# Sparse attention and a gated feed-forward layer on one core: attention products by 64 rows of one head, with dense keys and values

## The chip, the cores and the metric

The kernel runs on one NeuronCore of a Trainium2 chip. The core has five engines with a queue of instructions each: PE (TensorE, the matrix products; its weight loads are shown apart as PEld), DVE (VectorE), ACT (ScalarE), POOL (GpSimd) and SP (SyncE, which here only starts DMAs). PE writes into PSUM, which has 8 banks of 2 KB in each of 128 partitions. The metric is the device time of one execution in microseconds (us). Each number below is from three executions or from one profiled execution.

## What is computed

Eight batches, eight heads, 576 tokens, 64 numbers per head. In heads 0 to 3 a query sees the 32 tokens up to itself ("local"), in heads 4 to 7 the tokens whose position has the same remainder by 32 ("strided"). The result, 4608 tokens of 512 numbers, goes through a layer with 2048 hidden units:

```python
scores = scale * np.matmul(q, k.transpose(0, 1, 3, 2))
mask_local = (rel >= 0) & (rel < stride)                       # stride = 32
mask_strided = (rel >= 0) & (pos[None, :] % stride == pos[:, None] % stride)
scores = np.where(masks, scores, -1e9); attn = softmax(scores)
x = np.matmul(attn, v)                     # back to tokens x 512
h = x @ w_in
out = (h * (1 / (1 + np.exp(-h)))) @ w_out
```

## The kernel before

**Attention.** Two heads of one kind go together. A batch has six groups: three local (12 tiles of 32 queries, of both heads) and three strided (8, 8 and 6 tiles of 54 queries: three remainders of 18 tokens). A group has these steps, with the letters used below: S, the scores (L357, PE); M, mask, maximum and sign (L373, DVE), with the exponentials (L380, ACT; in the first two batches U on POOL, L389, and E on ACT, L393); R, sums and reciprocals (L398 to L400, DVE), and N, the scaling of a strided group (L404, DVE); T, transposes of 128x128 (L410, PE), and P, their copy to SBUF (L414, ACT); O, the products with the values (L422 local, L430 strided, PE). A local group goes on with Q, the division (L440, DVE), X, three transposes back (L460, PE), and B, a copy into `xb` (L465, ACT); of a strided group B sorts straight out of PSUM into `xb` (L453, ACT).

Both heads lie on the 128 partitions, and the keys and the values of a tile are spread out as a block diagonal with zeros: `kbd` is 128 x (2 x 64), and one product of 128 rows gives the scores of both heads. The zeros are written once at the start (L193 to L198 on DVE and POOL, L201 on ACT), and only then may keys and values be loaded between them, by two DMAs each (L315, L321). The output of a local product lies on 32 of PE's columns, that of a strided one on 64, so four or two of them, with different columns, can be under way at once. In float32 a product leaves two records in the trace (two weight loads and two matmuls), a transpose one.

**Feed-forward.** Nine blocks of 512 tokens, each of 16 chunks of 128 hidden units. A chunk is 12 matmuls of `hidden` (L492), tanh and gate (L502, L506), a split into a high and a low part (L514, L518), and 12 matmuls of `output` (L538), which come one chunk later. Every number is split into two float32r parts, and three products of them are summed. The input `x` of a block is split the same way (L480, L484) into one tile for each half, with a single place: the split of the next block stands after the last `hidden` of a block.

**Order.** PE's order is the program's. The first part (attention of batches 0 and 1, block 0, and the splitting of the weights, which arrive as 8-byte floats in 32 pieces of 512 KB) is put in order by a planner (`Steps.arrange`), which gives each step a cost per engine and a due time, and counts PSUM places ("rings"). From block 1 on the order is written out: after six of a block's 16 chunks `between` does T of group c+1, X of group c-1, S of group c+2, O of group c, R of group c+2. All of these and `hidden` take their PSUM banks in turn from a pool of four (`ps`); the other four (`po`) hold the sums of `output`. The groups of a batch run in the order local, local, local, strided, strided, strided.

Of the kernel before, what the change touches and what calls it, by code (L numbers as in the profile page):

```python
# [28 lines left out]
P = 128  # L29
# [11 lines left out]

KW = 64
# [4 lines left out]
VBUFS = 2  # L47

# [3 lines left out]


# [27 lines left out]


# [3 lines left out]
SIGNAL = 0.2  # L86

# [9 lines left out]
class Steps:  # L97
# [27 lines left out]
    def ready(self, step):  # L125
# [6 lines left out]
        for ring in step.takes:  # L132
            if len(self.taken[ring]) >= self.rings[ring]:
                for other in self.taken[ring][-self.rings[ring]].ends[ring]:
# [3 lines left out]
        return at  # L138

    def arrange(self):  # L140
        free = collections.defaultdict(float, SP=1.3, DVE=6.0, ACT=7.6, POOL=6.8)
        left, order = list(self.all), []
        while left:
# [9 lines left out]
            step.start, step.end, step.cost = at, at + cost, cost  # L153
            free[step.engine] = step.end
# [8 lines left out]
def sparse_attention_ffn(ctx: ExitStack, tc: tile.TileContext, kqt, vt, w_in, w_out, out):  # L163
# [12 lines left out]
        (1, 0, 12): "stage0", (1, 0, 14): "stage1", (1, 1, 12): "stage2", (1, 1, 14): "stage3",  # L176
        (1, 0, 9): "vbd2", (1, 1, 9): "zeros", (1, 0, 7): "kbd2",
# [8 lines left out]
    const.tile([P, 64], F32, name="pad1")  # L186
    zeros = const.tile([P, VT * D], F32, name="zeros")
# [11 lines left out]
    for vbd in vbds[1:]:  # L199
        for h in range(2):  # L200
            nc.scalar.copy(out=vbd[:, h], in_=zeros)  # L201
    vbds = [vbd.rearrange("p h (t d) -> p h t d", d=D) for vbd in vbds]
# [26 lines left out]
    make_identity(nc, ident)  # L229
# [5 lines left out]
    const.tile([P, 96], F32, name="pad3")  # L235
# [5 lines left out]
    def weight(layer, half, fc):  # L241
# [4 lines left out]
        if key not in places:  # L246
            places[key] = const.tile([P, n, DM], F32R, name=lent.get(key, "w%d%d_%d" % key))
# [64 lines left out]
    def load_qk(b, gi):  # L312
        n = max(GROUPS[gi].nq, GROUPS[gi].nk)
        for h in range(2):
# [3 lines left out]
    def load_v(b, gi):  # L318
        n = GROUPS[gi].count
        for h in range(2):  # L320
            load(out=vbds[gi % (VBUFS if b else VBUFS + 1)][h::2, h, :n], in_=vt[b, gi, h::2, :n])  # L321

# [7 lines left out]
    class Attention:  # L330


        def __init__(self, b, gi):
            self.b, self.gi, self.g = b, gi, GROUPS[gi]
            g = self.g
            self.kbd = kbds[gi % (KBUFS if b else KBUFS + 1)]
            self.vbd = vbds[gi % (VBUFS if b else VBUFS + 1)]
# [6 lines left out]
            self.quick = NG * b + gi < 2 * NG + 2  # L344
# [6 lines left out]

        def scores(self):
            g, kbd = self.g, self.kbd
            self.pss = self.bank("pss")
            s_ps = self.pss.rearrange("p (c h k) -> p c h k", h=2, k=KW)
# [143 lines left out]
    def tanh(ph, cols=slice(0, T), th=None):  # L499
        if th is None:  # L500
            th = ffn.tile([P, T], F32, name="th", bufs=1)
# [346 lines left out]
```

## Time and profile before

| | us |
|---|---|
| median of three executions (lowest, highest) | 936.03 (935.22, 936.04) |
| the profiled execution, its own time | 937.39 |
| its span from first to last instruction | 935.6 |
| PE busy | 916.1 (98%) |
| DVE busy | 431.8 (46%) |
| ACT busy | 322.6 (34%) |
| POOL busy | 19.0 (2%) |
| the chain of work that ended last: on PE | 91% |
| mean clock granted to PE, of full speed | 0.992 |

The profile is of one execution, and its own time lies 1.4 us above the median. A duration of one matmul (390 ns) is longer than the distance to the next one (227 ns), since matmuls overlap; so a stretch of PE's work is measured from its first start to the next stretch's first start. [...]

### The profile page before, as it was taken

What the parts mean: (1) busy time and instruction counts of PE and PEld (TensorE: products, weight loads), DVE (VectorE), ACT (ScalarE), POOL (GpSimd) and SP (SyncE); (2) the same over time, 40 slices, a digit from 0 to 9 for tenths busy, and PEclk for the clock granted to TensorE, in tenths of its full rate; (3) what the DMA queues carried; (4) which work ended last, traced back from release to release, by engine and by line L of the source; (5) the groups of instructions that cost most, each with busy time, mean ns of one, the idle gap of its engine ahead of it and who ended that gap; (6) DMA issues with size and microseconds to landing.
All of it is one profiled execution on the core that took longest, in us unless ns stands there. A gap on an engine that the chain in (4) does not pass through costs nothing.

```text
span 935.6 us, 15127 instructions
## 1 busy us (share of the span) xinstructions
PE 916.1 (98%) x5896; PEld 747.7 (80%) x5896; DVE 431.8 (46%) x1379; ACT 322.6 (34%) x915; POOL 19.0 (2%) x39
## 2 busy tenths in 40 slices
PE   6899999999999999999999999999999999999997
PEld 4687878888888888888888888888888888888886
DVE  7898754533544444433444344434343343343332
ACT  4877633323423233223432252233332131112112
POOL 4001000000000000000000000000000000000000
PEclk9799999999999999999999999999999999999999
DMA  7875522101301112102211121011210010001001
GB/s 237 287 254 182 179 77 82 57 29 45 109 27 39 56 37 94 45 29 72 82 48 38 36 91 55 30 58 44 82 38 9 1 46 1 1 0 46 1 1 45
DMA packets 36486, 62.85 MB, mean 67 GB/s; under 512 B 4160, under 2 KB 23616, under 8 KB 36416
## 3 DMA queue, kind: packets, MB, share of 16 engines
q1 hardware_dynamic: 36416, 61.90, 20.5%
q8 instruction: 46, 0.75, 0.3%
q14 instruction: 24, 0.20, 0.1%
HBM read 52.45 MB, written 9.44 MB: 66 GB/s over the span
## 4 chain that ended last, share of the span: by engine, by line
PE 91%; DVE 3%; DMA 3%; ACT 2%; issue 0%; SPq 0%; ACTq 0%
PE ps L492 41%; PE po L538 39%; PE ps L357 4%; PE ps L430 2%; PE ps L422 2%; DMA kbd<-kqt 2%; PE ps L410 2%; DVE xlo L484 1%; DMA stage<-w_in 1%; PE ps L460 1%; DVE glo L518 1%; ACT th L502 0%; ACT xhi L480 0%; DVE ghi L514 0%; ACT stage L256 0%
## 5 line engine op out<-in xcount | busy, mean ns | idle before, releaser
L492 PE MATMUL ps<-xhi,w 128*128 128x512 f32 x1152 | 387.6, 396 | 1.8 <-ACT pt L414 1.8
L506 DVE SCALAR_TENSOR_TENSOR th<-th,ps 128x512 f32<-128x512 f32 (+1 forms) x147 | 99.4, 676 | 350.1 <-ACT th L502 349.2
L492 PEld LDWEIGHTS ps<-xhi,w 128*128 128x128 f32 x1152 | 217.2, 189 | 51.8 <-issue 3.2
L502 ACT ACTIVATE th<-ps 128x512 f32<-128x512 f32 (+1 forms) x147 | 86.5, 589 | 459.6 <-PE ps L492 457.9
L492 PE MATMUL ps<-xlo,w 128*128 128x512 f32 x576 | 226.3, 393 | 0.3
L538 PE MATMUL po<-w,ghi 128*128 128x512 f32 x576 | 183.5, 390 | 0.4 <-DVE ghi L514 0.4
L492 PEld LDWEIGHTS ps<-xlo,w 128*128 128x128 f32 x576 | 108.7, 189 | 24.8 <-DVE xlo L484 3.4
L538 PEld LDWEIGHTS po<-w,ghi 128*128 128x128 f32 x576 | 108.0, 188 | 23.1 <-DVE ghi L514 0.6
L518 DVE TENSOR_TENSOR glo<-th,ghi 128x512 fp32r<-128x512 f32 (+1 forms) x147 | 100.1, 681 | 11.1 <-ACT ghi L514 0.4
L538 PE MATMUL po<-w,glo 128*128 128x512 f32 x252 | 98.2, 390 | 0.5 <-DVE glo L518 0.5
L538 PE MATMUL po<-stage,ghi 128*128 128x512 f32 x288 | 88.7, 389 | 0.0
L380 ACT ACTIVATE sm<-sm,sums 128x64 f32<-128x64 f32 x228 | 76.8, 341 | 17.3 <-DVE sums L373 17.3
L514 DVE CAST ghi<-th 128x512 fp32r<-128x512 f32 (+1 forms) x138 | 58.1, 421 | 11.3 <-PE po L538 0.5
L538 PEld LDWEIGHTS po<-stage,ghi 128*128 128x128 f32 x288 | 54.1, 188 | 11.4
L538 PE MATMUL po<-stage,glo 128*128 128x512 f32 x144 | 56.1, 390 | 0.0
L538 PEld LDWEIGHTS po<-w,glo 128*128 128x128 f32 x252 | 47.3, 188 | 10.8 <-DVE glo L518 0.9
L357 PE MATMUL ps<-kbd 128*32 128x128 f32 (+1 forms) x928 | 47.8, 292 | 8.0 <-POOL ident masks.py:197 5.1
L357 PEld LDWEIGHTS ps<-kbd 128*32 128x32 f32 (+1 forms) x928 | 35.0, 125 | 17.8 <-issue 11.1
L414 ACT COPY pt<-ps 128x384 f32<-128x384 f32 (+1 forms) x42 | 21.6, 513 | 79.4 <-PE ps L410 79.4
L380 ACT ACTIVATION_READ_ACCUMULATOR sm<-sm,sums 128x1 f32 x228 | 42.9, 188 | 0.0
L373 DVE CUSTOM_DVE_ANT_0 sm<-ps,mask_strided 128x64 f32<-128x64 f32 x176 | 27.3, 220 | 33.3 <-PE ps L357 33.3
L538 PE MATMUL po<-vbd,ghi 128*128 128x512 f32 x108 | 42.1, 390 | 0.0
(81 smaller groups left out, 769.7 us busy)
## 6 DMA issues: line engine op xcount, KB each, us to landing
vbd<-vt SPq DMA_DIRECT2D x48, 192.0 KB, 3.3
out<-osb SPq DMA_DIRECT2D x36, 256.0 KB, 2.1
stage<-w_in SPq DMA_DIRECT2D x16, 512.0 KB, 4.4
stage<-w_out SPq DMA_DIRECT2D x16, 512.0 KB, 4.8
kbd<-kqt SPq DMA_DIRECT2D x32, 221.0 KB, 3.3
kbd<-kqt SPq DMA_DIRECT2D x32, 208.0 KB, 3.0
vbd<-vt SPq DMA_DIRECT2D x32, 128.0 KB, 2.7
kbd<-kqt SPq DMA_DIRECT2D x16, 224.0 KB, 3.2
```

The costliest lines, as they stand in the source:

```text
L357: nc.tensor.matmul(s_ps[rows, c], kbd[:, 1, g.q0[t] : g.q0[t] + g.rows], kbd[:, 0:3:2, g.k0[t] : g.k0[t] + KW], start=True, stop=True,)
L373: nc.vector.tensor_tensor_reduce(out=s_sb[:, c, h], in0=s_ps[:, c, h], in1=masks[g.local, g.starts[c]][:, :KW], scale=-SCALE, scalar=BIG, ...
L380: nc.scalar.activation(out=s_sb[:, c, h], in_=s_sb[:, c, h], func=AF.Exp, bias=nmax[:, c, h : h + 1], scale=-1.0, accum_out=rsum[:, c, h : ...
L410: nc.tensor.transpose(self.psp[:, at], self.sm[:, at], ident)
L414: nc.scalar.copy(out=self.pt[:, : self.cols], in_=self.psp[:, : self.cols])
L422: nc.tensor.matmul(o_ps[rows, c], pt[:, c * P + rows.start : c * P + rows.stop], vbd[:, :, t], start=True, stop=True,)
L492: nc.tensor.matmul(ph, weight(0, wi, fc)[:, cc * P : (cc + 1) * P], x[xi][:, cc], start=(cc, n) == (0, 0), stop=(cc, n) == (NP - 1, 2),)
L502: nc.scalar.activation(out=th[:, cols], in_=ph[:, cols], func=AF.Tanh, scale=0.5)
L506: nc.vector.scalar_tensor_tensor(out=th[:, cols], in0=th[:, cols], scalar=1.0, in1=ph[:, cols], op0=ALU.add, op1=ALU.mult,)
L514: copy[engine](out=g[0][:, cols], in_=th[:, cols])
L518: nc.vector.tensor_sub(out=g[1][:, cols], in0=th[:, cols], in1=g[0][:, cols].bitcast(F32))
L538: nc.tensor.matmul(po[tt], g[gi][:, cols], weight(1, wi, fc), start=fc == 0 and n == 0, stop=fc == NFC - 1 and n == 2,)
```

## The change

1. **Dense keys and values.** `kbd` becomes `k` of 2 x 448 columns (keys, queries), with one head on partitions 0 to 63 and the other on 64 to 127; `vbd` becomes `v`. There are no zeros to write, and one DMA of 128 partitions loads a group's keys and queries or its values. Batch 0 has four places for keys and six for values (before: three and three).
2. **Products by 64 rows.** S has two products of 64 rows and 64 columns for each tile in place of one of 128 rows and 128 columns, and the two heads write into two banks. O of a local group likewise, with two banks; O of a strided group keeps its number of products, with 64 rows in place of 128, in one bank. Q becomes two instructions. P and the B of a local group may go to ACT or DVE in the planned part.
3. **Order.** From batch 1 on the groups alternate: local, strided, local, strided, local, strided. `between` does O before S.
4. **x in more places.** Each 128 of the 512 inputs has a tile of its own, six places in all; the first two are split after chunk 14, the others after chunk 15. `th` has two places.
5. **Idle products.** The planner fills PE's gaps of over 0.4 us in the first 60 us of its plan with transposes of the identity (L639), so many as it reckons to fit.

```diff
-    vbds = [const.tile([P, 2, VT * D], F32, name=f"vbd{i}") for i in range(VBUFS + 1)]
-    kbds = [const.tile([P, 3, QW], F32, name=f"kbd{i}") for i in range(KBUFS + 1)]
+    vbds = [const.tile([P, 2, VT, D], F32, name=f"v{i}") for i in range(0, VFIRST, 2)]
+    kbds = [const.tile([P, 2, QW], F32, name=f"k{i}") for i in range(KFIRST)]
-    nc.vector.memset(kbds[0][:, 0], 0.0)
-    nc.gpsimd.memset(kbds[0][:, 2], 0.0)
-    nc.vector.memset(kbds[1][:, 0:3:2], 0.0)
-    nc.vector.memset(vbds[0], 0.0)
-    nc.vector.memset(zeros, 0.0)
-    nc.vector.memset(kbds[2][:, 0:3:2], 0.0)
...
-        for h in range(2):
-            load(out=kbds[gi % (KBUFS if b else KBUFS + 1)][h::2, h : h + 2, :n],
-                 in_=kqt[b, gi, h::2, :, :n])
+        load(out=kbds[kbd_of(a.b, a.at)][:, :, :n], in_=kqt[a.b, a.gi, :, :, :n])
...
         def scores(self):
-            self.pss = self.bank("pss")
+            self.pss = [self.bank("pss") for _ in range(2)]
             for t, c, rows in self.tiles:
-                nc.tensor.matmul(
-                    s_ps[rows, c], kbd[:, 1, g.q0[t] : g.q0[t] + g.rows],
-                    kbd[:, 0:3:2, g.k0[t] : g.k0[t] + KW], start=True, stop=True,
-                )
+                for h in range(2):
+                    at = slice(h * D, (h + 1) * D)
+                    nc.tensor.matmul(
+                        self.pss[h][rows, c * KW : (c + 1) * KW],
+                        kbd[at, 1, g.q0[t] : g.q0[t] + g.rows],
+                        kbd[at, 0, g.k0[t] : g.k0[t] + KW], start=True, stop=True,
+                    )
...
         def values(self):
+                    if g.local:
+                        nc.tensor.matmul(
+                            self.pso[h][rows, c * D : (c + 1) * D],
+                            pt[at, p0 : p0 + g.rows], vbd[at, t], start=True, stop=True,
+                        )
+                    else:
+                        nc.tensor.matmul(
+                            self.pso[h * D : (h + 1) * D, t * SEQ : (t + 1) * SEQ], vbd[at, t],
+                            pt[at, p0 : p0 + SEQ], start=True, stop=True,
+                        )
...
+def order_of(b):
+    return range(NG) if b == 0 else (0, 3, 1, 4, 2, 5)
...
     def between(k, fc):
             turn(c + 1)
             back(c - 1)
+            values(c)
             scores(c + 2)
-            values(c)
             total(c + 2)
...
+    def idle(n):
+        bank = ps.tile([P, 512], F32, name="ps")
+        for i in range(n):
+            nc.tensor.transpose(bank[:, i % 4 * P : (i % 4 + 1) * P], ident, ident)
...
-            if fc == NFC - 1 and k + 1 < NBLK:
-                x = new_x()
-                for cc in range(NP):
-                    x_high(k + 1, x, cc)
-                    x_low(k + 1, x, cc)
             output(*lag, po)
...
+            if fc >= NFC - 2 and k + 1 < NBLK:
+                if fc == NFC - 2:
+                    x1 = new_x()
+                for cc in range(NP // 2) if fc == NFC - 2 else range(NP // 2, NP):
+                    x_high(k + 1, x1, cc)
+                    x_low(k + 1, x1, cc)
```

What the change moves, first on PE from block 1 on. Before, in a place where O and S are of different kinds (a row is one product or a run of equal ones, 32x128 is the output, the waits in brackets name the semaphores by engine, DMAHW being a DMA):

```order
L410 MATMUL ps<-ident,sm 128x128 x2
L357 MATMUL ps<-kbd_80 32x128 [waits DMAHW7_49,DMAHW4_49]
L357 MATMUL ps<-kbd_80 32x128 x11
L430 MATMUL ps<-pt,vbd_77 64x54 [waits DMAHW5_49]
L430 MATMUL ps<-pt,vbd_77 64x54 [waits DMAHW6_49]
L430 MATMUL ps<-pt,vbd_77 64x54 x14
```

After, in a place with a local group c:

```order
L438 MATMUL ps<-ident,sm 128x128 [waits PE_49,Activation_49]
L438 MATMUL ps<-ident,sm 128x128 [waits Activation_49] x2
L455 MATMUL ps<-v_77,pt 32x64 [waits DMAHW6_49]
L455 MATMUL ps<-v_77,pt 32x64 x23
L384 MATMUL ps<-k_80 32x64 [waits DMAHW7_49,DVE_49]
L384 MATMUL ps<-k_80 32x64 [waits Activation_49]
L384 MATMUL ps<-k_80 32x64 x22
L525 MATMUL ps<-xhi,w_0_616 128x512 [waits DVE_49]
```

O (L455) now stands ahead of S (L384) and is of the same kind; S has 24 products for 12; its first product waits for DVE, and its second, which takes the other bank, waits for ACT.

At the program's start, SP's queue before, for the keys of groups 0 to 2, the first values and the second keys of `kbd_80`:

```order
L315 DMA kbd_80<-kqt 64x2x416 [waits DVE_49]
L315 DMA kbd_80<-kqt 64x2x416 [waits Pool_49]
L315 DMA kbd_81<-kqt 64x896 [waits DVE_49]
L315 DMA kbd_81<-kqt 64x896
L315 DMA kbd_82<-kqt 64x2x416 [waits DVE_49]
L315 DMA kbd_82<-kqt 64x2x416
L321 DMA vbd_77<-vt 64x768 x2
L315 DMA kbd_80<-kqt 64x2x442 [waits DMAHW0_49,PE_49]
```

And after, to the first piece of the weights:

```order
L340 DMA k_80<-kqt 128x2x416
L340 DMA k_81<-kqt 128x896
L340 DMA k_82<-kqt 128x2x416
L344 DMA v_77<-vt 128x768
L340 DMA k_83<-kqt 128x2x442
L344 DMA v_77<-vt 128x768
L340 DMA k_80<-kqt 128x2x442 [waits DMAHW0_49,PE_49]
L344 DMA v_78<-vt 128x768
L340 DMA k_81<-kqt 128x2x334 [waits DMAHW1_49,PE_49]
L344 DMA v_78<-vt 128x512
L312 DMA stage_428<-w_in 128x4x256 [waits DMAHW2_49]
```

The waits for the zeros of DVE and POOL are gone from SP's queue, and half of its instructions for keys and values.

## Rows read from the trace of the kernel before

**Rows 1.** The page: busy time (us, share, instructions) and the last chain by line.

```profile
PE 916.1 (98%) x5896; PEld 747.7 (80%) x5896; DVE 431.8 (46%) x1379; ACT 322.6 (34%) x915; POOL 19.0 (2%) x39
PE ps L492 41%; PE po L538 39%; PE ps L357 4%; PE ps L430 2%; PE ps L422 2%; DMA kbd<-kqt 2%; PE ps L410 2%; DVE xlo L484 1%; DMA stage<-w_in 1%; PE ps L460 1%; DVE glo L518 1%; ACT th L502 0%; ACT xhi L480 0%; DVE ghi L514 0%; ACT stage L256 0%
```

**Rows 2.** Stretches: us; busy by PE, PEld, DVE, ACT, POOL; PEclk; DMA share, GB/s.

```profile
13.20:23.44 10.24, 7.52 (x123) 5.34 (x112) 7.88 (x55) 5.08 (x11) 2.78 (x3) 1.00 0.93 291
23.44:28.55 5.11, 3.01 (x36) 2.50 (x36) 4.55 (x12) 4.49 (x8) 0.13 (x1) 0.50 1.00 340
28.55:33.68 5.13, 5.00 (x62) 4.35 (x63) 2.67 (x6) 2.74 (x7) 0.00 (x0) 0.50 0.88 340
...
43.92:47.34 3.42, 3.42 (x10) 2.65 (x9) 3.42 (x17) 2.95 (x7) 0.84 (x1) 0.50 0.95 325
...
60.00:77.70 17.70, 16.87 (x130) 13.00 (x128) 14.98 (x43) 13.35 (x25) 0.84 (x1) 1.00 0.71 232
...
246.41:348.71 102.30, 102.25 (x691) 83.82 (x689) 43.30 (x154) 34.46 (x121) 0.00 (x0) 1.00 0.18 55
```

**Rows 3.** The chain that ended last, two pieces of block 0: start, us, what.

```profile
91.04 2.72 PE po L538 x12
93.76 2.72 PE ps L492 x12
```

**Rows 4.** Timeline of PE in blocks 1 and 2: start, us, engine, line, operation, count.

```profile
146.85 0.49 PE L410 MATMUL ps<-ident,sm 128*128 128x128 f32 x3
147.27 0.86 PE L357 MATMUL ps<-kbd 128*32 128x128 f32 x24
147.95 0.84 PE L422 MATMUL ps<-vbd,pt 128*32 128x128 f32 x24
148.72 0.50 PE L492 MATMUL ps<-xhi,w 128*128 128x512 f32 x1
...
197.91 0.60 PE L410 MATMUL ps<-ident,sm 128*128 128x128 f32 x4
...
198.78 0.88 PE L357 MATMUL ps<-kbd 128*64 128x128 f32 x12
199.48 1.09 PE L430 MATMUL ps<-pt,vbd 128*64 128x54 f32 x32
200.50 0.50 PE L492 MATMUL ps<-xhi,w 128*128 128x512 f32 x1
...
230.69 0.86 PE L357 MATMUL ps<-kbd 128*32 128x128 f32 x24
231.49 0.91 PE L430 MATMUL ps<-pt,vbd 128*64 128x54 f32 x24
```

**Rows 5.** Timeline of ACT, two copies P in the same places.

```profile
147.38 0.48 ACT L414 COPY pt<-ps 128x384 f32<-128x384 f32 x1 [1.10 <-PE ps L410]
...
198.56 0.59 ACT L414 COPY pt<-ps 128x512 f32<-128x512 f32 x1 [2.57 <-PE ps L410]
```

**Rows 6.** Weight loads alone in a stretch: us, PEld busy (count), PEclk, DMA share, GB/s.

```profile
28.67:28.75 0.08, 0.08 (x8) 0.50 1.06 422
```

**Rows 7.** The chain that ended last, pieces from the start to 33 us.

```profile
4.82 0.82 DVE kbd L198
...
5.65 0.63 SPq L315
...
22.02 6.53 DMA kbd<-kqt
...
28.68 1.51 PE ps L357 x24
30.19 1.89 PE po L430 x32
32.08 0.85 PE po L410 x3
```

**Rows 8.** Timeline of PE: the first matmul of the feed-forward layer.

```profile
32.57 0.78 PE L492 MATMUL ps<-xhi,w 128*128 128x512 f32 x1
```

More of the change, by code (lines that the diff above doesn't have):

```diff
@@ L131, in ready @@
             at = max(at, other.end + (SIGNAL if other.engine != "SP" else LANDING))
-        for ring in step.takes:
-            if len(self.taken[ring]) >= self.rings[ring]:
-                for other in self.taken[ring][-self.rings[ring]].ends[ring]:
+        for ring in set(step.takes):
+            taken = self.taken[ring]
+            last = len(taken) + step.takes.count(ring) - self.rings[ring]
+            for before in taken[max(0, last - step.takes.count(ring)) : max(0, last)]:
+                for other in before.ends[ring]:
                     if other.end is None:
@@ L138, in ready, with keep_warm @@
         return at
+    def keep_warm(self, start, end):
+        n = int((end - start - 0.1) / (COLD if end < WARM_FROM else WARM))
+        taken, size = self.taken["ps"], self.rings["ps"]
+        if end - start < 0.4 or n < 1:
+            return []
+        if len(taken) >= size:
+            ends = [other.end for other in taken[-size].ends["ps"]]
+            if None in ends or max(ends) > start:
+                return []
+        step = Step("idle", {}, 0, [], lambda: self.idle(n))
+        step.engine, step.start, step.end, step.cost = "PE", start, end - 0.1, end - start
+        step.ends["ps"] = [step]
+        taken.append(step)
+        return [step]
     def arrange(self):
-        free = collections.defaultdict(float, SP=1.3, DVE=6.0, ACT=7.6, POOL=6.8)
+        free = collections.defaultdict(float, PE=1.6, SP=1.3, DVE=2.0, ACT=4.0, POOL=6.8)
         left, order = list(self.all), []
@@ L153, in arrange @@
             step.start, step.end, step.cost = at, at + cost, cost
+            if step.engine == "PE" and at < WARM_UNTIL:
+                order += self.keep_warm(free["PE"], at)
             free[step.engine] = step.end
@@ L410, in turn, with turned @@
                 nc.tensor.transpose(self.psp[:, at], self.sm[:, at], ident)
-        def turned(self):
+        def turned(self, engine="ACT"):
             self.pt = att.tile([P, 512], F32, name="pt")
-            nc.scalar.copy(out=self.pt[:, : self.cols], in_=self.psp[:, : self.cols])
+            copy[engine](out=self.pt[:, : self.cols], in_=self.psp[:, : self.cols])
         def values(self):
             g, pt, vbd = self.g, self.pt, self.vbd
-            self.pso = pso = self.bank("pso")
             if g.local:
-                o_ps = pso.rearrange("p (c h d) -> p c h d", h=2, d=D)
-                for t, c, rows in self.tiles:
-                    nc.tensor.matmul(
-                        o_ps[rows, c], pt[:, c * P + rows.start : c * P + rows.stop], vbd[:, :, t],
-                        start=True, stop=True,
-                    )
-                return
+                self.pso = [self.bank("pso") for _ in range(2)]
+            else:
+                self.pso = self.bank("pso")
             for t, c, rows in self.tiles:
@@ L460, in back, with done @@
                 nc.tensor.transpose(self.psx[:, at], self.xq[:, at], ident)
-        def done(self):
+        def done(self, engine="ACT"):
             flat = place_of(self.b).rearrange("p n s -> p (n s)")
             x0 = self.g.first * STRIDE
-            nc.scalar.copy(out=flat[:, x0 : x0 + self.cols], in_=self.psx[:, : self.cols])
+            copy[engine](out=flat[:, x0 : x0 + self.cols], in_=self.psx[:, : self.cols])
     def new_x():
-        return [ffn.tile([P, NP, T], F32R, name=n, bufs=1) for n in ("xhi", "xlo")]
+        return [[None] * NP for _ in range(2)]
     def parts(k, cc):
```

160 lines of the change are left out of this document (82 added, 78 removed), and 3 rows, old and new, of the table lent.

## The prediction

> **What bounds the kernel now.** I read the page's busy times and its last chain first: PE is busy for 916 of 935.6 us, and the chain runs on L492 and L538 (41% and 39%), with the attention products L357, L430, L422 and the transposes behind them [rows 1]. Next the table of stretches: from block 1 on a block takes 102.30 us in which PE is busy for 102.25 (the five blocks from 144.12 us on read alike), while DVE works 43 and ACT 34 of them [rows 2]. So there PE's own work is the time. Before 77.7 us that isn't so: PE has gaps, the clock falls to 0.50 twice, and DVE and the DMAs are the busiest [rows 2]. The change has therefore two places, to be priced apart.
>
> What a block holds: 12 matmuls take 2.72 us [rows 3], a chunk 5.44, 16 chunks 87.04. The other 15.26 us are one batch's attention, six places of `between`. The timeline shows how they go: 24 records of a local S run from 147.27 to 147.95 (0.68 us, four at once on different columns, six rounds of about 0.11), the 12 records of a small strided S take 0.70 (two at once, again six rounds of 0.11), a local O 0.77 to the first L492, of which 0.66 are rounds and 0.11 the change back to full products. A strided O with 54 columns has 16 rounds in 1.02 - 0.11 us, 0.057 each. Where O is of the other kind than S, S takes 0.80 in place of 0.68 [rows 4].
>
> **The change, part by part.**
>
> *Products by 64 rows.* S has twice the products, each with half the columns. If products on the lower and the upper 64 rows run at once, as those on different columns do now, a round has eight records (local) or four (strided) and half the columns. The nearest row for a round of so few columns is the strided O: 0.057 us. The number of rounds stays: in a block 18 for local S, 18 for local O, 22 for strided S (8, 8, 6), in all 58. They save 58 x (0.11 - 0.057) = 3.07 us. The strided O keeps its 44 rounds of two, so nothing. The ends of this price: 0.057 with overlap, 0.114 without. I take overlap, since nothing in the timeline treats one part of the array differently from another, but no row shows it for rows; see the rivals.
>
> *Alternating kinds, O before S.* O of c and S of c+2 are now always of one kind. Before, four of six places had different kinds: 4 x (0.80 - 0.68) = 0.48 us saved in a block [rows 4]. What else moves in these places: the load of the values is issued ahead of that of the keys on SP, Q ahead of M on DVE, and the sorting copy B ahead of the exponentials on ACT. Nobody is late by that: DVE and ACT are idle for over half of a block [rows 2], and the next place is at least two chunks (10.9 us) off.
>
> *The new wait.* A place takes five banks in turn out of the four of `ps`: with a local O these are T, O, O, S, S. The second bank of S is the one that T used, so S waits for the copy P (its second product waits for ACT). P ends 1.24 us after the first of four transposes, or 1.01 after the first of three [rows 4, 5]. PE gets to S after T (0.42 for three and the change of mode, 0.53 for four) and O (6 x 0.057 = 0.34): at 0.76 or 0.87. It waits 0.25 or 0.37 us; 2 x 0.37 + 0.25 = 1.0 us in a block. Behind it in PE's queue stand `hidden` and everything else, so all of it counts. In the places with a strided O (T, X, O, S, S) PE needs about 1.7 us to S, and P is done. The next `hidden` takes O's first bank, which Q's first half frees: Q starts when O ends and runs while S waits and runs, so I cost that at nothing; if DVE were late there, at most Q's 0.55 x 3 a block.
>
> *x in six places, th in two.* PE is idle for 0.05 us in a block [rows 2]: there is nothing to gain; at nothing. In the other direction the cast of the last quarters still stands ahead of the last tanh on ACT, covered by 2.72 us of `output`.
>
> So a block saves 3.07 + 0.48 - 1.0 = 2.55 us, and the six blocks with attention behind them (1 to 6) 15.3. In block 0 the attention of batch 1 shrinks too, but PE is the bound only in the later part: half, 1.3.
>
> *The start.* The zeros are gone: the third load of keys waited on SP for L198 until 5.65 us [rows 7]. The load that decides is that of the keys of batch 1's first group: it ends at 28.55, PE waits for it with S, and S, a strided O and T (28.68 to 32.57) stand ahead of the first L492 [rows 7, 8]. In SP's order the bytes up to it are the same (by the tiles' shapes, 4 bytes a number), 2.56 MB of keys and queries, 1.90 of values, three pieces of 0.52 and 0.43 for itself: 6.46 MB, at the 291 GB/s of 13 to 23 us [rows 2] 22.2 us. From 2 us on, that ends near 24.2: 4.3 us earlier. DVE must follow: between 13.20 and 33.68 it has 5.4 us idle [rows 2], of which the copies P and B and the second half of Q, now also its work, take some 1.5, leaving 3.9, close to 4.3. I take 4.3; the ends are 2 (DVE or weights late) and 6.5 (S, O and T at full clock as well: 3.9 us that at 1.00 would be about 2.1).
>
> *Idle products.* 28.55 to 33.68 and 43.92 to 47.34 ran at 0.50, both after gaps of PE [rows 2]. In the second PE was busy throughout, so half of 3.42 us was lost there, 1.7. With PE kept busy, and a first stretch without that gap, I take half: 0.85. They lie in gaps, so cost nothing, unless the planner's gap isn't one.
> [...]
>
> **The sum.** 15.3 + 1.3 + 4.3 + 0.85 = 21.8 us off the profiled execution's 937.4, so 915.6; the profiled execution lies 1.4 above the median 936.0, which gives 914.2.
>
> **The rivals.**
>
> *The two halves of a strided O take turns* (930). They write different partitions of the same bank, from different rows. If PE can't do that at once, its 44 rounds go from 0.057 to 0.114: 2.5 us a block, 16 us with block 0's half. Against it: today's two products of a round share a bank too, though from the same rows [rows 4].
> [...]
>
> *Rows don't overlap at all* (947, slower). Products on different rows take turns everywhere. S and the local O need 58 x 0.114, as long as now (+0.2), the strided O +2.5, the kinds give back 0.48, P is no longer waited for: +2.3 us a block, 6.5 blocks' worth 14.7; the start gives 4 back. The point that decides: a round of 0.13 us eats all gains (58 x 0.02 - 0.48 is 0.8 us a block, 5.2 in all, what the start saves). For it: the trace shows overlap of columns alone.
>
> *PE's sequencer can't feed it* (955, slower). A local place now has 96 records for 48. The fastest that the trace sustains is 24 records in 0.66 us, 0.0275 each [rows 4]; if this were the sequencer's pace and not the rounds', S and O would take 1.32 us each, +0.66 x 6 - 0.48 = 3.5 us a block. Against it: after a wait for a DMA, with nothing queued, eight weight loads start within 0.08 us [rows 6], 0.010 each; at that pace a local S takes 0.48, 917 in all.
>
> *The start gives nothing* (919): the weights, or DVE with its copies, or idle products in a gap that isn't one hold back what the loads give; the blocks gain the same.
>
> **How the numbers follow.** Chances: the forecast 0.64, its own range 903 (no wait for P, 6.5 us at the start, the whole 1.7 of the clock) to 923 (0.010 us a record, 2 us at the start); no gain at the start 0.08; halves of a strided O in turn 0.10; no overlap of rows 0.10; the sequencer 0.08. The range 903 to 931 leaves out the last two. A measurement of this kernel can tell about 0.2% (1.9 us) from no change. Faster is the first three, 0.82, slower the last two without a rest in between, 0.16, same 0.02.
>
> **What would show it.** In blocks 1 to 5 the block should take 99.7 us; a local S 0.34 us plus the change of mode, with records seven to eight in a burst; ACT P as what ended a wait of 0.25 to 0.37 us at S, three times in a block; a strided O still near 1.0 (2.0 would be the bank rival); bursts of four and blocks of 104 us the no-overlap rival; records evenly some 0.027 us apart the sequencer. The first feed-forward matmul should start near 28 us, and the clock should stay at 1.00 from some point before 15 us. The forecast is wrong if the blocks don't shrink by at least 2 us each, whatever the start does.

## The result: 922.8 us for 935.6, and the profile after

The changed kernel takes 922.83 us (median of four executions, 922.16 to 923.33), the kernel before, run beside it, 935.62 (933.48 to 936.04): a ratio of 0.9873, 95% interval 0.9855 to 0.989. So it is 1.3% faster. The time lies in the range given; the forecast of 914.2 (2.3%) was 8.6 us too low. The profiled execution took 923.33 us (span 921.5), 14.1 less than the profiled one of before, where the sum had said 21.8.

The page: busy time, and the chain by line, to be read against [rows 1].

```profile
PE 904.5 (98%) x7451; PEld 742.9 (81%) x7451; DVE 436.6 (47%) x1408; ACT 315.1 (34%) x897; POOL 19.0 (2%) x38
PE ps L525 39%; PE po L571 39%; PE ps L384 3%; PE ps L460 2%; DMA stage<-w_in 2%; PE ps L438 1%; PE ps L455 1%; DVE stage L287 1%; DVE w L327 1%; DVE glo L551 1%; DVE sm L402 1%; PE ps L491 1%; DMA stage<-w_out 1%; DVE th L539 1%; PE ps L639 1%; ACT stage L276 1%
```

In the new numbering S is L384, T L438, P L442, O L455 (local) and L460 (strided), X L491, `hidden` L525, `output` L571, the idle transposes L639; M is L402, Q L471, R L425 to L429, N L432. PE has 11.6 us less work; the chain still runs through the feed-forward matmuls. Stretches (us; PE, PEld, DVE, ACT, POOL busy; PEclk; DMA share, GB/s), cut at the first L525 and at block boundaries, where blocks were cut before too [rows 2] (a boundary is the start of the `output` matmuls that stand behind a block's first `hidden`):

```profile
0.00:29.32 29.32, 24.75 (x568) 21.08 (x569) 18.93 (x113) 13.65 (x25) 10.44 (x30) 0.94 0.81 292
29.32:60.00 30.68, 28.99 (x221) 22.29 (x220) 30.48 (x90) 25.86 (x47) 3.29 (x3) 1.00 0.74 238
60.00:100.00 40.00, 38.16 (x409) 29.76 (x409) 35.08 (x102) 24.86 (x45) 3.32 (x3) 1.00 0.59 189
100.00:141.71 41.71, 39.83 (x312) 30.86 (x311) 28.25 (x79) 18.25 (x36) 0.83 (x1) 1.00 0.37 119
141.71:243.74 102.03, 100.19 (x878) 82.62 (x877) 46.60 (x171) 35.47 (x122) 1.14 (x1) 1.00 0.17 55
243.74:343.70 99.96, 99.96 (x879) 82.75 (x877) 44.07 (x157) 34.74 (x121) 0.00 (x0) 1.00 0.17 56
```

Subtracting the boundaries of the two traces gives the account of the 14.1 us:

| stretch | before | after | gain | forecast |
|---|---|---|---|---|
| to the first matmul of `hidden` | 32.57 | 29.32 | 3.25 | 4.3 |
| from there to block 1's boundary (with the clock's 0.85) | 111.54 | 112.39 | -0.85 | 2.15 |
| block 1 | 102.30 | 102.03 | 0.27 | 2.55 |
| blocks 2 to 5, each | 102.30 | 99.95 | 2.35 | 2.55 |
| block 6 | 100.43 | 98.51 | 1.92 | 2.55 |

The steady blocks do nearly what was forecast. Half of the shortfall lies before block 1's boundary and 2.3 us in block 1, where PE is idle for 1.84 us (102.03 less 100.19). The last 4.45 us before that boundary (137.26 to 141.71; 2.88 before) are the first `hidden` of block 1; for 1.0 us of them PE waits for the split of x on DVE.

Timeline of PE and ACT in a steady block of after (start, us, engine, line, operation, count), a local place, to be read against [rows 4, 5]:

```profile
346.43 0.60 PE L438 MATMUL ps<-ident,sm 128*128 128x128 f32 x4
346.95 0.72 PE L455 MATMUL ps<-v,pt 64*32 64x64 f32 x48
347.48 0.93 PE L384 MATMUL ps<-k 64*32 64x64 f32 x48
348.33 0.50 PE L525 MATMUL ps<-xhi,w 128*128 128x512 f32 x1
```

```profile
347.06 0.59 ACT L442 COPY pt<-ps 128x512 f32<-128x512 f32 x1 [1.20 <-PE ps L438]
```

O takes 0.53 us from its start to that of S (forecast 0.34), S 0.85 to the next L525. Its third record starts at 347.70, right behind the end of the copy P at 347.65: the new wait is there, though the table of waits doesn't list it: it lies between two records of one group. A strided place:

```profile
365.54 1.07 PE L460 MATMUL ps<-pt,v 64*64 64x54 f32 x29
...
366.50 0.65 PE L384 MATMUL ps<-k 64*64 64x64 f32 x30
367.08 0.50 PE L525 MATMUL ps<-xhi,w 128*128 128x512 f32 x1
```

The strided O takes 0.96 us up to S's run (1.02 before, with the change to full products [rows 4]; in turns it would be near 2), so its halves don't take turns. S of eight tiles takes 0.58 with that change (before 1.03, with a change of kind). Last, the start of block 1, PE and DVE, with the T of its first place (recorded expectations below call it the second):

```profile
140.44 0.50 PE L525 MATMUL ps<-xlo,w 128*128 128x512 f32 x1 [0.83 <-DVE xlo L517]
...
144.21 0.39 PE L571 MATMUL po<-stage,glo 128*128 128x512 f32 x1
146.44 0.63 PE L438 MATMUL ps<-ident,sm 128*128 128x128 f32 x4 [1.84 <-DVE sm L432]
```

```profile
143.84 0.69 DVE L551 TENSOR_TENSOR glo<-th,ghi 128x512 fp32r<-128x512 f32 x1
144.44 0.68 DVE L425 TENSOR_REDUCE sums<-sm 128x8 f32<-128x512 f32 x1
...
145.60 0.69 DVE L432 TENSOR_TENSOR sm<-sm,sums 128x512 f32<-128x512 f32 x1
```

Group 13, second of its batch, was local and is now strided. T of a strided group needs N, and that stands on DVE behind the group's own M, the split of x and a gate: PE, with everything behind T in its queue, waits 1.84 us.

### The profile page after: what moved, and what is told of

Its sections match the earlier page's. It is cut to its first block, busy times and chain, and to the rows that moved or that the text cites. A ratio compares the mean times of both kernels' runs of the same rounds, so it can differ in the third digit from the quotient of the medians.

```text
span 921.5 us, 18028 instructions
## 1 busy us (share of the span) xinstructions
PE 904.5 (98%) x7451; PEld 742.9 (81%) x7451; DVE 436.6 (47%) x1408; ACT 315.1 (34%) x897; POOL 19.0 (2%) x38
## 4 chain that ended last, share of the span: by engine, by line
PE 87%; DVE 7%; DMA 3%; ACT 2%; issue 0%; ACTq 0%; SPq 0%
PE ps L525 39%; PE po L571 39%; PE ps L384 3%; PE ps L460 2%; DMA stage<-w_in 2%; PE ps L438 1%; PE ps L455 1%; DVE stage L287 1%; DVE w L327 1%; DVE glo L551 1%; DVE sm L402 1%; PE ps L491 1%; DMA stage<-w_out 1%; DVE th L539 1%; PE ps L639 1%; ACT stage L276 1%
## 5 line engine op out<-in xcount | busy, mean ns | idle before, releaser
L525 PE MATMUL ps<-xhi,w 128*128 128x512 f32 x1152 | 386.6, 395 | 2.2 <-DVE th L539 1.5
L525 PEld LDWEIGHTS ps<-xhi,w 128*128 128x128 f32 x1152 | 216.2, 188 | 50.5 <-DVE th L539 1.9
L539 DVE SCALAR_TENSOR_TENSOR th<-th,ps 128x512 f32<-128x512 f32 (+1 forms) x147 | 99.3, 675 | 319.2 <-ACT th L535 319.1
L525 PE MATMUL ps<-xlo,w 128*128 128x512 f32 x576 | 225.2, 391 | 1.7 <-DVE xlo L517 1.7
L571 PE MATMUL po<-w,ghi 128*128 128x512 f32 x504 | 155.4, 390 | 0.7 <-ACT ghi L547 0.7
L525 PEld LDWEIGHTS ps<-xlo,w 128*128 128x128 f32 x576 | 108.2, 188 | 23.8 <-DVE xlo L517 3.0
L571 PEld LDWEIGHTS po<-w,ghi 128*128 128x128 f32 x504 | 94.4, 188 | 20.4 <-ACT ghi L547 0.8
L571 PE MATMUL po<-w,glo 128*128 128x512 f32 x252 | 98.3, 390 | 0.3 <-DVE glo L551 0.3
L571 PE MATMUL po<-stage,ghi 128*128 128x512 f32 x288 | 88.7, 389 | 0.0
L571 PE MATMUL po<-v,ghi 128*128 128x512 f32 x216 | 66.7, 390 | 0.0
L571 PEld LDWEIGHTS po<-stage,ghi 128*128 128x128 f32 x288 | 54.1, 188 | 11.3
L571 PEld LDWEIGHTS po<-w,glo 128*128 128x128 f32 x252 | 47.3, 188 | 11.0 <-DVE glo L551 1.2
L571 PE MATMUL po<-stage,glo 128*128 128x512 f32 x144 | 56.1, 389 | 0.0
L442 ACT COPY pt<-ps 128x384 f32<-128x384 f32 (+1 forms) x40 | 20.6, 514 | 79.8 <-PE ps L438 79.8
L571 PEld LDWEIGHTS po<-v,ghi 128*128 128x128 f32 x216 | 40.4, 188 | 8.5 <-ACT ghi L547 0.2
L571 PE MATMUL po<-k,ghi 128*128 128x512 f32 x144 | 44.3, 389 | 0.0
L571 PE MATMUL po<-v,glo 128*128 128x512 f32 x108 | 42.2, 391 | 0.4 <-DVE glo L551 0.4
```

The lines of the kernel that those rows point to most:

```text
L442: copy[engine](out=self.pt[:, : self.cols], in_=self.psp[:, : self.cols])
L525: nc.tensor.matmul(ph, weight(0, wi, fc)[:, cc * P : (cc + 1) * P], x[xi][cc], start=(cc, n) == (0, 0), stop=(cc, n) == (NP - 1, 2),)
L539: nc.vector.scalar_tensor_tensor(out=th[:, cols], in0=th[:, cols], scalar=1.0, in1=ph[:, cols], op0=ALU.add, op1=ALU.mult,)
L571: nc.tensor.matmul(po[tt], g[gi][:, cols], weight(1, wi, fc), start=fc == 0 and n == 0, stop=fc == NFC - 1 and n == 2,)
```

## The experiments

All are edits of the changed kernel, compared with the kernel before on the same chip. The theory: in the blocks local products are held by how fast PE is fed and by the wait for P; in block 1 by the wait for N; before that by DVE. Rivals stand with each.

**The wait for P, and for N.**

```diff
     def between(k, fc):
-            turn(c + 1)
...
             between(k, fc)
+            if (k, fc - 1) in plan:
+                turn(plan[k, fc - 1] + 1)
```

> The transposes T of group c+1 with their copy P go from their place in the program to one chunk later (also one place alone), so that O and S have banks that nobody has to empty first. Theory A (S really waits for P's bank): a local S takes 0.65 us for 0.86, three times a block, so blocks 2 to 5 take about 99.3 us for 99.95; and the stall of 2.0 us at 144.2 us, where T waits for the sums and the scaling of a strided group in block 1, goes too: about 917 us for 922.8. Rival B (the wait lies over time in which PE's sequencer makes up its lead of weight loads, and is paid back by a slower S): blocks stay within 0.2 us of 99.95, and only the stall in block 1 goes: about 920.5. Rival C (T alone pays a change of mode more, twice 0.1 us a place): blocks 100.5 us, 923 to 925.

917.44 us (917.11 to 918.74), ratio 0.9811 (0.9786 to 0.9835): Theory A's total. Block 1 takes 99.80, its stall is gone. But blocks 2 to 5 take 99.65, between A and B. The places show why: O and S together take 1.18 us for 1.38, so the wait was 0.20 us (0.10 in the place with three transposes). All attention work of a block, T alone included, takes 10.7 us for 12.0. But of these 1.3 us 1.0 comes back in the products next to it, 0.17 at each of six places, where T alone now changes from and to full products.

**T later only where S waits.**

```diff
-            turn(c + 1)
+            if not groups[c].g.local:
+                turn(c + 1)
...
             between(k, fc)
+            if (k, fc - 1) in plan and groups[plan[k, fc - 1]].g.local:
+                turn(plan[k, fc - 1] + 1)
```

> T of group c+1 and its copy P come one chunk later only in the places where O is that of a local group (three of six in a block); in the others T stays where the change has it. Theory A (in a local place S waits 0.1 to 0.2 us for P, and T alone costs 0.16 us for its own change from and to full products): by the run with T later everywhere, where blocks took 99.65 us, a local place gains 0.38, 0.38 and 0.27 less 0.16 each, and the strided places lose nothing: blocks 99.95 - 0.55 = 99.4 us, the stall at 144.2 us gone with the clock's dip that followed it in some runs: about 916 us, ratio 0.979 to 0.981. Rival B (the gain of that run came from the stall in block 1 alone): blocks 99.8 to 100, about 918.5. Rival C (the strided places gained there too): blocks 99.65 again.

916.98 us (916.76 to 917.07), ratio 0.9803 (0.979 to 0.9817), blocks 99.50, block 1 99.67: A, 0.1 us a block short. PE in a local place, then T alone, and the block:

```profile
341.67 0.67 PE L455 MATMUL ps<-v,pt 64*32 64x64 f32 x44
...
342.18 0.71 PE L384 MATMUL ps<-k 64*32 64x64 f32 x44
342.83 0.50 PE L525 MATMUL ps<-xhi,w 128*128 128x512 f32 x1
...
348.41 0.60 PE L438 MATMUL ps<-ident,sm 128*128 128x128 f32 x4
348.76 0.48 PE L525 MATMUL ps<-xhi,w 128*128 128x512 f32 x1
```

```profile
239.36:338.86 99.50, 99.50 (x879) 82.12 (x877) 43.79 (x157) 34.72 (x121) 0.00 (x0) 1.00 0.18 57
```

From 341.67 to 342.83 are 1.16 us for O and S, with no gap: without any wait they still take more than the 0.34 + 0.34 + 0.11 forecast. The blocks are 0.45 us shorter than the changed kernel's and 0.15 shorter than with T later everywhere; the totals of the two runs with T later, 916.98 and 917.44 us, were not measured side by side, and their intervals overlap.

**O before T**, another way to spare P's bank.

```diff
-            turn(c + 1)
             back(c - 1)
             values(c)
+            if c != 2 * NG:
+                turn(c + 1)
             scores(c + 2)
...
+            if (k, fc) == (1, 1):
+                turn(2 * NG + 1)
```

> The changed kernel with O of group c before T of group c+1 in a place (order X, O, T, S), so that the banks go O, O, T, S, S and S's second bank is one that Q empties, not the one that P empties; only T of group 13 comes one chunk later. Theory A (S waits for the copy P): a local place, O, T and S, takes about 0.53 + 0.45 + 0.65 = 1.63 to 1.70 us for 1.91, blocks 99.3 to 99.45, the stall at 144.2 gone, total 922.8 - 2.0 - 3.3 = 917.5. Rival B (a change between transposes and products within the place costs as much as the wait): blocks 99.9 to 100.2, total 921. Rival C (S then waits for Q's first half on DVE, 0.55 us after O): local places stay at 1.9.

927.74 us, ratio 0.9927 (0.9908 to 0.9947), blocks 101.29: Rival B, and worse. A local place:

```profile
347.79 0.72 PE L455 MATMUL ps<-v,pt 64*32 64x64 f32 x48
348.45 0.66 PE L438 MATMUL ps<-ident,sm 128*128 128x128 f32 x4
349.03 0.72 PE L384 MATMUL ps<-k 64*32 64x64 f32 x48
349.69 0.50 PE L525 MATMUL ps<-xhi,w 128*128 128x512 f32 x1
```

O takes 0.66 for 0.53 and S 0.66: the wait for P is gone, and two changes of kind took its place (1.90 for 1.91); the strided places, which had no wait, lose 0.3 each.

**Kinds.**

```diff
-    return range(NG) if b == 0 else (0, 3, 1, 4, 2, 5)
+    return range(NG)
```

> The changed kernel with the groups of a batch in the old order (three local, then three strided); O still before S. The prediction's step: four of six places again have O and S of different kinds, 4 x 0.12 = 0.48 us a block, blocks 100.4 us for 99.95. Theory on block 1: its second place has a local group again, T needs no scaling, and the stall of 2.0 us at 144.2 us goes, so that the total is 922.8 - 2 + 6 x 0.48 = 923.7. Rival (a change of kind costs nothing once O stands before S, since a place with O and S of different kinds lets the lead of the weight loads be made up): blocks within 0.1 us of 99.95, the total near 920.8.

924.22 us, ratio 0.9884 (0.985 to 0.9918). The stall in block 1 is gone (100.30), but steady blocks take 100.8 to 101.2. Two places with O and S of different kinds:

```profile
366.17 0.72 PE L455 MATMUL ps<-v,pt 64*32 64x64 f32 x48
366.83 0.73 PE L384 MATMUL ps<-k 64*64 64x64 f32 x32
368.03 0.50 PE L525 MATMUL ps<-xhi,w 128*128 128x512 f32 x1 [0.48 <-DVE xq L471]
```

A local O takes 0.66 for 0.53, so the change of kind costs 0.13 (the step had 0.12); and with T, X, O, O, S, S a place takes six banks, and the next `hidden` waits 0.48 us for Q. Alternating is worth about 1.0 us a block (0.85 to 1.2, this wait for a bank included), twice what the prediction gave it, less 2 us once.

**How fast PE can be fed.**

```diff
+        forms = {1: (2, 64, 24), 2: (2, 32, 24), 3: (2, 128, 24), 4: (1, 64, 24), 5: (0, 64, 24),
+                 6: (2, 64, 48)}
...
+            nc.tensor.matmul(
+                banks[h][r : r + 32, c * cols : (c + 1) * cols], ident[at, r : r + 32],
+                ident[at, :cols], start=True, stop=True,
+            )
```

By block: how many halves (0 for all 128 rows), columns, products.

> The changed kernel with additional products whose results nobody reads, after chunks 2 and 9 of blocks 1 to 6, each with 32 columns of output: block 1: 24 products of 64 rows, alternately lower and upper half, 64 columns long; block 2: the same with 32 columns; block 3: with 128; block 4: 24 of the lower half alone, 64 columns; block 5: 24 of all 128 rows, 64 columns; block 6: 48 as in block 1. Theory A (after a lead of about 16 weight loads PE's sequencer gives a record only every 0.0165 us): blocks 1, 2 and 5 take the same 0.5 to 0.55 us for their 48 records, block 6 0.8 us more. Theory B (the array sets it, rows overlapping): block 1 takes 6 rounds of 0.057 = 0.34, block 2 half of that, block 3 twice, block 4 twice block 1, block 6 twice block 1. Theory C (rows do not overlap): blocks 1 and 4 and 5 alike, with 32 columns half.

Timeline of PE, the additional products of blocks 1, 2, 4 and 6 (a product is two records):

```profile
157.51 0.72 PE L816 MATMUL ps<-ident 64*32 64x64 f32 x48
158.17 0.50 PE L525 MATMUL ps<-xhi,w 128*128 128x512 f32 x1
...
259.26 0.62 PE L816 MATMUL ps<-ident 64*32 64x32 f32 x48
259.81 0.50 PE L525 MATMUL ps<-xhi,w 128*128 128x512 f32 x1
...
463.00 0.88 PE L816 MATMUL ps<-ident 64*32 64x64 f32 x48
463.80 0.50 PE L525 MATMUL ps<-xhi,w 128*128 128x512 f32 x1
...
667.10 1.17 PE L816 MATMUL ps<-ident 64*32 64x64 f32 x96
668.20 0.50 PE L525 MATMUL ps<-xhi,w 128*128 128x512 f32 x1
```

From first record to L525, the change to full products included: 0.66 for two halves, 0.55 with 32 columns, 0.80 for the lower half alone (block 4) and for all 128 rows (block 5), 0.87 with 128 columns, and 1.10 for twice as many as in block 1. None of the three theories holds with its numbers. Rows do overlap (0.66 against 0.80), so C falls. But eight at once are not twice as fast as four, and half the columns save 0.11 of 0.66, so B falls. The 48 records more of block 6 cost 0.44 us, 0.0092 each, not A's 0.0165. On one half, 0.80 less the change of 0.11 is twelve rounds of 0.057, the price that the prediction gave a round. On both halves that price holds only at first: the first 32 records of block 6 start in four bursts of eight, 0.055 to 0.08 us apart (with 128 columns 0.11 to 0.13), and from the 33rd on records come singly or by twos. What stands: behind the first 32 a run of small products on both halves took 0.009 us a record or more, and 32 columns in place of 64 saved 0.11 us of 0.66.

**DVE in block 0**: the subtraction of the weights' low part moved to POOL, and, apart from it, made twice for half of the pieces.

```diff
-        nc.vector.tensor_sub(
+        {"DVE": nc.vector, "POOL": nc.gpsimd}[engine].tensor_sub(
...
```

> The changed kernel with the subtraction that gives the low part of the 32 weight pieces (L327) on POOL in place of DVE: 27 x 0.73 = 19.5 us of DVE's 109 before 137 us go to POOL, which works 18 of them. Theory A (DVE bounds the start and block 0: 30.5 of 30.7 us busy between 29.3 and 60): the first chunks of block 0 come earlier, block 1's boundary at 141.7 comes 2 to 4 us earlier, total 919 to 921. Rival B (the weights come as fast as their two stage places and the DMAs let them; a POOL subtraction takes 1.35 us by its 1.01 us for 128x384, so the places come free later): boundary 141.7 to 144, total 923 to 925. Blocks 2 to 8 unchanged in both, 99.95.

933.77 us, ratio 0.9997 (0.9985 to 1.0009): the whole gain is gone, and block 1's boundary comes at 149.8. B's direction, but not its size. Groups on DVE up to 147 us, of the changed kernel and then of this one (busy us, mean ns of one):

```profile
L287 DVE SCALAR_TENSOR_TENSOR stage<-stage 128x512 int32<-128x512 int32 x32 | 22.7, 723 | 4.5 <-ACT stage L281 4.3
L323 DVE CAST w<-stage 128x512 fp32r<-128x512 f32 x9 | 3.7, 419 | 0.0
```

```profile
L287 DVE SCALAR_TENSOR_TENSOR stage<-stage 128x512 int32<-128x512 int32 x32 | 31.4, 996 | 5.5 <-ACT stage L281 5.3
L323 DVE CAST w<-stage 128x512 fp32r<-128x512 f32 x13 | 10.1, 781 | 0.1
```

The time that DVE gave away came back as longer operations beside POOL, so the run doesn't decide on its theory. The next tells more:

```diff
+        for _ in range(2 - i % 2):
             nc.vector.tensor_sub(
```

> The changed kernel with the subtraction for the low part of every second weight piece made twice on DVE, with the same result: 16 x 0.73 = 11.7 us more for DVE before 137 us, nothing more for any other engine, the order planned as without them. Theory A (DVE sets the pace of block 0 until about 100 us): most of it comes through, the boundary at 141.7 us (138.3 to 141.7 in the profiles of kernels with this first part) moves to 148 to 153, the total is 930 to 934. Rival B (the stage places and the DMAs of the weights set it, DVE merely looks full): under 3 us come through, total 922 to 926. Rival C (PE sets it, as the prediction had it for the later half): the first half of block 0 gets later and PE makes it up, total within 2 us.

929.87 us, ratio 0.9935 (0.9911 to 0.9959), 7 us more than the changed kernel; the boundary comes at 147.9, 5 to 9 later than in the eight profiles with the same first part (138.6 to 142.5). Block 0, read as [rows 2]:

```profile
29.30:60.00 30.70, 28.58 (x207) 21.81 (x206) 30.11 (x79) 23.07 (x40) 2.46 (x2) 0.89 0.68 216
60.00:100.00 40.00, 36.12 (x344) 27.78 (x343) 38.31 (x105) 23.45 (x42) 3.02 (x3) 0.96 0.55 171
```

That is a little below A's ends and far from B and C: DVE's work comes through. But it doesn't come through as waiting alone. From the first `hidden` to the boundary PE is idle for 8.3 us, 3 to 4 more than in the two profiles of the changed kernel (5.4 and 3.9), and its busy time is 4.5 to 5 us longer, which fits the clock: it stood at 0.50 from 33.97 to 40.80 and from 88.59 to 92.00, behind gaps of PE, and half of PE's 9.4 busy us there is 4.7 (an estimate). In those two profiles it is at 1.00 throughout the stretch, and PE is busy for 95 to 96% of it. So DVE holds PE up in block 0; that it alone sets the pace isn't shown.

**Idle products.**

```diff
-        if end - start < 0.4 or n < 1:
+        if True:
```

> The changed kernel without the idle transposes. Theory A (they lie on the chain: 11 of them took 2.54 us at the half clock from 20.14 us on, and X at 22.68 stands behind them): the first feed-forward matmul starts 1 to 2 us earlier than 29.3, the total is 921 to 922. Rival B (they keep the clock up, as the prediction had it, 0.85 us): more stretches at 0.50 than the one from 19.8 to 23.2, the total 923.5 to 925. Rival C (DVE and the weights hold back block 0 whatever PE does): the first matmul moves, the start of block 1 at 141.7 doesn't, the total within 0.5 us of 922.8.

924.54 us (922.54 to 926.02), ratio 0.9878 (0.9845 to 0.9911): in the total not to be told from the changed kernel. The profile (which took 925.67) shows what they do:

```profile
22.09:32.33 10.24, 8.78 (x128) 7.35 (x129) 8.81 (x28) 8.46 (x17) 1.12 (x1) 0.50 0.62 196
32.33:42.57 10.24, 8.31 (x85) 5.93 (x84) 10.03 (x29) 8.60 (x16) 1.12 (x1) 1.00 0.68 232
42.57:45.98 3.41, 3.41 (x10) 2.64 (x9) 3.34 (x16) 2.01 (x5) 0.00 (x0) 0.50 0.87 262
```

Without them the clock is at 0.50 for 10.24 and again for 3.41 us, and `hidden` starts at 31.65; with them at 28.3 to 30.3 (eight profiles), with 0.50 for at most 6.8 us before 25. The mean clock of its four executions is 0.990 to 0.994, that of the changed kernel's eight 0.994 to 0.999. So A falls: they don't hold back the chain, and they keep the clock up, as B says. That this gains little in the end fits C, but no run shows why.

**Smaller parts.**

```diff
-XBUFS = NP + 2
+XBUFS = NP
...
+            if fc == NFC - 1 and k + 1 < NBLK:
+                x = new_x()
+                for cc in range(NP):
+                    x_high(k + 1, x, cc)
+                    x_low(k + 1, x, cc)
             output(*lag, po)
...
```

> The changed kernel with the split of x as it was: all four quarters after the last hidden of a block, four places. The prediction priced this part at nothing: 0.05 us of idle PE in a block. By the traces the stall of 0.21 us at the block's boundary (245.0 us before, gone after) was its share: then blocks 2 to 6 take 100.16 us for 99.95, and the one at 141.7 loses a little, total 924 to 924.5. Rival (the stall went with the order of O and S or with alternating kinds, not with x): blocks 99.95, total within 0.3 of 922.8.

921.30 us, ratio 0.9864 (0.985 to 0.9879), blocks 99.97: the rival by the blocks; the total is 1.5 us lower than it said, but the ratios can't be told apart. Splitting earlier and in more places gives nothing. The run isn't the split of before in full: it keeps a tile for each 128 inputs, where before had one for each half.

```diff
-        p = add(f"P{c}", {"ACT": 0.05 + 0.13 * n, "DVE": 0.08 + 0.14 * n}, t1 + 0.5, [t],
+        p = add(f"P{c}", {"ACT": 0.05 + 0.13 * n}, t1 + 0.5, [t],
...
```

> The changed kernel with the copies P and the local B of the planned part on ACT alone, as before the change (about 5 copies of 0.5 us leave DVE before 137 us). Theory A (DVE's added copies took part of the start's gain): the first feed-forward matmul or block 1's boundary 0.5 to 2.5 us earlier, total 920.5 to 922.3. Rival B (a copy on ACT waits behind casts of 0.67 us, and transposes and O wait for it; the change to either engine was worth having): 0.5 to 2 us later, 923.3 to 925.

922.25 us, ratio 0.9875 (0.986 to 0.989). The time lies at A's upper end, `hidden` starts at 28.5 and the boundary comes at 138.3, but the unaltered start gave 28.3 to 30.3 and 138.6 to 142.5: no effect of the copies' engine can be told from that scatter.

The kernel with T later in local places and x as before:

> As the one with T later in local places, and x split as before the change (four places, all after a block's last hidden). Theory A (the split of x in six places gives nothing): within 0.5 us of that kernel, blocks within 0.02 us of it. Rival B (the split ahead of the last chunk disturbs ACT and DVE, as the 1.5 us between the two medians of 922.8 and 921.3 would have it): 1 to 1.5 us less. Rival C (without the stall in block 1 the block's boundary wait of 0.2 us comes back): blocks 0.2 us longer, 1.2 us more in all.

917.83 us (915.5 to 918.99), ratio 0.9811 (0.9796 to 0.9826), blocks 99.49: A by the blocks, which are the same to 0.01; the total is 0.85 us above that kernel's, more than A's 0.5 but within its own scatter. Nothing from the earlier split.

**The changed kernel again.**

> The changed kernel once more, unaltered, beside the two others. If the 3 us by which the start of block 1 differs between profiles of kernels with the same first part (138.3 to 141.7 us) is chance of the start (how long PE waits for its instructions near 17 us, and whether the clock dips), then this profile has block 1's boundary anywhere from 138 to 142 and a stall of about 2 us at its second place, steady blocks 99.95 to 99.97, and a median of 921 to 923. If the profile shown first was the rule, the boundary comes at 141.7 again and the clock is at 0.50 from 19.8 to 23.2.

922.16 us (921.17 to 923.08), ratio 0.9859 (0.9845 to 0.9872). The boundary comes at 139.7, the stall in block 1's first place is there, steady blocks take 99.95. So 2 us of the first profile's block 0 were chance; by this one (29.36 to 139.69) its gain there is not -0.85 but 1.2. The run of T later in local places stands 5.2 us (0.6%) below this one, measured beside it.

## Why the prediction was right, and where it was off

*Steady blocks: right, 2.35 for 2.55, but by errors that cancel.* A strided O with an S of six rounds went from 1.73 [rows 4] to 1.43 us (397.20 to 398.63), 0.05 a round, as priced. A change of kind costs 0.13 us for 0.12. The wait for P is 0.20 us behind four transposes and 0.10 behind three, for 0.37 and 0.25. The local rounds were to save 12 x 0.053 = 0.64 us a place; O and S went from 1.45 [rows 4] to 1.18, which saves 0.27. This is the term that was mis-sized: the price of a round, 0.057, was taken from a strided O, which has two records in a round, and a local round of the change has eight. In the local O at 346.95 the first four rounds begin 0.05 to 0.08 us apart, near that price; the last 16 of its 48 records take 0.27 us, 0.017 each. Over O and S a round comes to 0.09. The rival of the sequencer named 0.010 us a record from [rows 6] and wrote "917 in all" beside it; that price (measured: 0.0092, and 0.011 in O and S) was the better one. It is the part of that rival which came true; its own pace of 0.0275 didn't. The smaller wait paid for part: PE was later at S. A leftover of 0.36 us a block is seen, nearly all of it at the block's boundary in the trace of before, where the matmuls at 245.14 and 245.48 us come 0.44 and 0.34 us after the one ahead, for 0.227 elsewhere: the first one's weight load waits for the split of x on DVE. The prediction had put this at 0.05. The wait stayed away when x was split late and in four places again; the tile for each 128 inputs wasn't taken back, so whether that closed it stays open. In the rival without overlap of rows 58 x 0.02 - 0.48 is 0.7, not 0.8; nothing hangs on it.

*"Nobody is late by that": wrong in block 1.* The step looked at steady blocks, where DVE is idle for half the time. At the seam between the planned part and the written order the new second group is strided, its T needs N, and DVE has hardly paused since 136.5 us (8.43 us busy of the 9.08 to 145.60). That costs 2.0 us, and with the clock down to 0.50 for 3.4 us behind the gap in some profiles (143.95 to 147.36 in the run with additional products).

*The start: near in size, but by another way.* 3.25 for 4.3; the eight profiles with this start have 28.3 to 30.3, so the forecast of 28 is their edge. The load that was to decide did come earlier: issued at 15.88 and 5.4 us under way, the keys of batch 1's first group were there at 21.3 (forecast 24.2, before 28.55). But their S no longer waits for them:

```profile
27.08 1.14 PE L460 MATMUL po<-pt,v 64*64 64x54 f32 x32
28.15 0.72 PE L384 MATMUL ps<-k 64*32 64x64 f32 x48
```

S, a strided O and T stand ahead of the first `hidden` in both kernels (now with O first): before from 28.68 to 32.57 at clock 0.50 [rows 2, 7, 8], now from 27.08 to 29.32 at 1.00. So 1.6 us come from the earlier start of the three, not 4.3, and 1.65 from their shorter run, which the sum had left to the upper end of the range. That the total came near is luck. Why they don't start before 27.08 wasn't taken apart. The clock dipped once here too, after a gap that the kernel before doesn't have:

```profile
16.43 0.52 PE L491 MATMUL po<-ident,xq 128*128 128x128 f32 x3 [0.64 <-DVE xq L471]
16.88 0.30 PE L455 MATMUL po<-v,pt 64*32 64x64 f32 x5
18.84 0.68 PE L455 MATMUL po<-v,pt 64*32 64x64 f32 x43 [1.66 <-issue]
...
20.07 2.61 PE L639 MATMUL ps<-ident 128*128 128x128 f32 x11
```

In the middle of one O, PE waits for nothing that the profile shows, 1.66 to 2.9 us in every profile of this start, always behind the fifth record of that O, which is the 347th matmul record in the trace. Without the idle products, of which 23 stand ahead of it, the stop (1.41 us) lies behind the 28th record of that O, again the 347th in the trace. So its place goes with the number of PE's instructions, not with a piece of data. A 16 KB transfer of the queue named "instruction" begins at 16.57, and in all these profiles PE goes on 2.2 to 2.6 us after the start of one. That PE waits for its own instructions, of which it now has more in less time, is inferred from the two; no run altered the transfer.

*Block 0: the waits were left out.* "PE is the bound only in the later part: half" priced the shorter products and the clock, not the waits. From the first `hidden` to block 1's boundary PE's busy time fell from 108.9 to 107.0 us (106.4 in the second profile), near the forecast of 2.15, but its idle time rose from 2.65 to 5.4 (3.9), nearly all of it in waits for DVE and ACT; 1.0 us of them stands in block 1's first `hidden`. How much of the 1.9 and 2.5 us less work is the attention's isn't shown: 4.5 us of this stretch ran at 0.50 before, and half of that, 2.3 (an estimate), would be enough. The gain was -0.85 and 1.2 in the two profiles, and boundaries of the same first part differ by 4 us.

*The rivals.* Strided halves in turn: no, O takes 0.96 us. No overlap of rows: no, 0.66 against 0.80. Nothing gained at the start: no, 3.25 us. With the idle transposes the mean clock stood higher, 0.994 to 0.999 for 0.990 to 0.994 without them.

## What to carry to other kernels

Price a burst of tiny products by records, not by what they overlap: past the first 32 or so they came 0.009 to 0.017 us apart here, and halving a product's rows and columns gained 0.27 us of the 1.45 of O and S in a local place. A change of order is to be followed through the seam where a planned part ends, not only through a steady block, and a wait for a bank is cured where it is (three places of six), since each step moved on its own paid a change of kind, 0.17 us here. Before an engine's shorter work is counted, double one operation on the engine suspected of setting the pace there, and split the delay into waiting and lost clock.

## What the runs showed of the hardware

*PE's first 32 records.* Starts of the 96 records above, by count in the first stretch (us; PE busy, count; clock):

```profile
667.10:667.33 0.23, 0.23 (x31) 1.00 0.00 0
```

31 begin in 0.23 us, 0.0074 each; the other 65 take 0.87 less 0.11, 0.0117 each. The local O of the changed kernel at 346.95 begins alike: 33 weight loads start in its first 0.20 us and 32 matmuls in 0.24; then the next loads come 0.08 and 0.06 us apart, the next matmuls 0.03 and 0.06. What sets the pace from there on, no run shows.

*DVE beside POOL.* With POOL working 65 of 145 us for 18 of 137, a join with two inputs in SBUF went from 723 to 996 ns in the mean and a cast from 419 to 781, while the gate (L539), which reads one of its two tiles from PSUM, stayed at 680 and 678. Why the gate was spared, no run shows.
